# Wrapped spectra of a lag kernel, summed by accumulating transfers into DRAM in place of GpSimd copies and sums

## The chip, the cores and the metric

The kernel runs on one core of one Trainium2 chip. The metric is the device time of one execution in microseconds (us). A core has TensorE (PE; its weight loads are listed as PEld), VectorE (DVE), ScalarE (ACT), GpSimd (POOL) and SyncE (SP), each with an in-order queue of its own, and sixteen DMA engines that all queues share. SP and POOL issue the transfers here.

## The reference

A block of four residual layers over x (2048 positions, 512 channels): A, B, A, B, with the same weights in both rounds, each on a normalized input.

```python
def _A_ref(u, A_re, A_im, B_re, B_im, C_re, C_im, log_dt, Dskip):
    dt = jnp.exp(log_dt)[:, None]
    logdA = dt * (A_re + 1j * A_im)
    dB = dt * (B_re + 1j * B_im)
    P = jnp.exp(logdA[:, :, None] * l[None, None, :])      # 512 x 128 x 2048
    K = jnp.einsum("dn,dnl,dn->dl", C, P, dB).real         # the lag kernel, 512 x 2048
    # causal convolution of u with K along the positions, by FFTs of length 4096
    ...
    return y + u * Dskip

def _B_ref(x, w_gate, w_up, w_down):
    return (silu(x @ w_gate) * (x @ w_up)) @ w_down        # 512 -> 1376 -> 512

for _ in range(2):
    x = x + _A_ref(layernorm(x), ...)
    x = x + _B_ref(layernorm(x), ...)
```

## The kernel before, in words

**Blocks of 512 positions.** The convolution is cut into four blocks of positions (NB = 4) and the lag kernel into four parts of 512 lags. A block's spectrum has 512 complex values per channel, held as four quarters q of 128 (partitions), each with a real and an imaginary plane. Output block b is the sum over k = 0 to b of input spectrum b - k times the lag kernel's spectrum k. Because a product of two blocks of 512 spills into the next block, the lag spectrum that is used for k over 0 is a *wrapped* one: the spectrum of part k plus or minus the other plane of the spectrum of part k - 1 (real: subtract, imaginary: add, for the even quarters; the signs change places for the odd ones). Spectrum 0 is used as it is. It stays in SBUF in `w0r`; spectra 1 to 3 go to DRAM in `wdr` and are loaded again (L732) wherever a block needs them.

**The lag kernel by chunks of 64 channels.** There are eight chunks. For each, DVE and ACT make tables of powers (`gen_turns`, `gen_reduce`, `gen_trig`, `gen_exp`, `gen_mags`, `gen_e`) and a factor `g` (`gen_g`); the second half of g is finished by two accumulating transfers of 512 KB, issued by POOL into SBUF (L494, L499). PE multiplies tables and g into the lags of the chunk (`lags`, L509 and L510), ACT copies them out (`spread_in`, L515), PE spreads them over the partitions (`spread`), and ACT copies that out (L1001). Then `spectra` takes them through a transform on PE, one quarter after the other.

**`spectra`, where the change is made.** For a quarter with all four parts (k0 = 0, 29 times) PE writes `pw` (PSUM, tag sml, four buffers), ACT copies it to `s1` (L555; SBUF, tag uu, three buffers), POOL copies part 0 to `w0r` (L557) and makes the wrapped sums `wo` (L563, two operations; tag sg, two buffers), and SP stores each of the three parts to DRAM (L569). For three quarters of the last two chunks only part 0 is made first (ACT straight to `w0r`, L551) and parts 1 to 3 later (k0 = 1, three times; POOL's L566 and L567). The tag uu is also that of the early input spectra `u` (L289) and of the loaded input spectra `uu` in the blocks (L734); the tag sg is also that of the feed-forward's `sg`.

**Order.** The chunks run in a software pipeline that is written by hand: the functions are generators, and a loop over i (L958 to L1026) takes so many steps of each. For ACT, DVE and PE this order is kept as written (`manual_schedule`); SP's and POOL's instructions are placed by the scheduler when they are ready in its own timeline. In one turn of the loop, PE and ACT finish quarters 3 and 4 of chunk i - 1, the lags of chunk i, and quarters 1 and 2 of chunk i; DVE makes tables and g of the next chunks. Beside this, norms of the weights are summed: `st` is loaded (L314), squared by ACT (L316) and summed by PE (L320). Behind the loop come the last chunk, the first block's products (L736 to L741), the splitting of the weights (L626, L632) and the first norm (L202 to L207); then blocks of `ssm` and `ffn` alternate until the end.

The generator's steps are taken as `take(sp, n)`: one step is a quarter's products on PE, the next its copies and stores.

Of the kernel before, what the change touches and what calls it, by code (L numbers as in the profile page):

```python
# [15 lines left out]
AF = mybir.ActivationFunctionType  # L16
OP = mybir.AluOpType
# [5 lines left out]
P = 128  # L23
T = 512
NB = L // T
# [9 lines left out]
DC = 64  # L35
# [46 lines left out]
def kernel(ctx, tc, x, a_re, a_im, b_re, b_im, c_re, c_im, log_dt, d_skip,  # L82
                           w_gate, w_up, w_down, c_ef, c_ei, c_ek, c_am, c_eh, c_eih, out):
    nc = tc.nc
    V, A, G, PE = nc.vector, nc.scalar, nc.gpsimd, nc.tensor
# [9 lines left out]
    def tl(shape, name, tag, dt=F32):  # L95
        return sb.tile(shape, dt, name=name, tag=tag, bufs=BUFS[tag])

    def pbig(shape, name):
        return ps.tile(shape, F32, name=name, tag="big", bufs=2)

    def psml(shape, name):
        return ps.tile(shape, F32, name=name, tag="sml", bufs=4)
# [29 lines left out]
    w0r = sb.tile([P, 2, 4, 2, HD], F32, name="w0r")  # L132
# [19 lines left out]
    wdr = dram.tile([NB, 2, 4, P, 2, HD], F32, name="wdr")  # L152
# [139 lines left out]
    def second(h, q, space=psml):  # L292
        n = []
        for cp in range(2):
            t = tl([P, 2, HD], "n1", "w")
            nc.sync.dma_start(t, ndr[h, cp])
            n += [t[:, 0], t[:, 1]]
        return direct(1, h, q, n, space)
# [232 lines left out]
    def spectra(ch, kt, k0, k1, qs=QORD):  # L531


        h, off = ch // 4, (ch % 4) * DC
        nk = k1 - k0
        for q in qs:
            if k1 == 1:
                pw = pbig([P, 2, 8, 4, 16], "pw")[:, :, 0:1]
            elif k0 == 1:
                pw = pbig([P, 2, nk, 4, 16], "pw")  # L540
            else:
                pw = psml([P, 2, nk, 4, 16], "pw")
            for i, c in [(i, c) for c in range(4) for i in range(2)] if k1 == 1 else \
                        [(i, c) for i in range(2) for c in range(4)]:
                e = ek[q // 2][:, q % 2, c - 1, i] if c else ef[:, q, i]
                PE.matmul(pw[:, i], lhsT=e, rhs=kt[:, :, c + 4 * k0:4 * k1:4, :].rearrange("p g k d -> p k g d"), start=c == 0, stop=c == 3)  # L546
                if k0 == 1 and (i, c) == (0, 3):
                    yield
            yield
            if k1 == 1:  # L550
                A.activation(w0r[:, h, q, :, off:off + DC].rearrange("p i (g d) -> p i g d", g=4), pw[:, :, 0], AF.Copy)  # L551
                yield
                continue
            s1 = tl([P, 2, NB, 4, 16], "s1", "uu")
            A.activation(s1[:, :, :nk], pw, AF.Copy)  # L555
            if k0 == 0:
                G.tensor_copy(w0r[:, h, q, :, off:off + DC].rearrange("p i (g d) -> p i g d", g=4), s1[:, :, 0])  # L557
            sp, np_ = s1, NB - 1
            wo = tl([P, 2, NB - 1, 4, 16], "wo", "sg")
            ops = (OP.subtract, OP.add) if q % 2 == 0 else (OP.add, OP.subtract)  # L560
            for i in range(2):
                if k0 == 0:
                    G.tensor_tensor(wo[:, i], s1[:, i, 1:], s1[:, 1 - i, :3], ops[i])  # L563
                else:
                    w0s = w0r[:, h, q, 1 - i, off:off + DC].rearrange("p (g d) -> p g d", g=4)
                    G.tensor_tensor(wo[:, i, 0], s1[:, i, 0], w0s, ops[i])  # L566
                    G.tensor_tensor(wo[:, i, 1:], s1[:, i, 1:3], s1[:, 1 - i, :2], ops[i])  # L567
            for k in range(1, NB):
                nc.sync.dma_start(wdr[k, h, q, :, :, off:off + DC].rearrange("p i (g d) -> p i g d", g=4),  # L569
                                  wo[:, :, k - 1])  # L570
            yield


    def sizes(ch, kt, junk):

        A.activation(junk, kt, AF.Abs, accum_out=wsum[:, ch:ch + 1])
# [18 lines left out]
    def take(it, n):  # L595
        for _ in range(n):
            next(it, None)
# [301 lines left out]
    with tc.manual_schedule(engines={mybir.EngineType.Activation, mybir.EngineType.DVE, mybir.EngineType.PE}):  # L899
# [57 lines left out]
        sp = iter(())  # L957
        for i in range(NCH - 1):  # L958
# [46 lines left out]
            if more:  # L1005
                sp = spectra(i, kt, 0, NB)
                take(sp, 1)
                ex = gen_exp(i + 2, ts[i + 2])
                take(ex, 100)
                mags = gen_mags(i + 2, ts[i + 2])  # L1010
                take(mags, 2)
                norm_units(3, 9)
                take(sp, 2)
                norm_units(0, 0)
                take(mags, 2)
                take(sp, 2)
                sizes(i, kt, ks)
                take(ge, 4)
                take(gg, 1)
                while tops:  # L1020
                    tops.pop(0)()
                ts[i] = gs[i] = None
            else:
                sizes(i, kt, ks)
                take(ge, 4)
                take(gg, 1)  # L1026
# [9 lines left out]
        spec, ahead = inputs(), []  # L1036
        first = ssm(0, 0)
        sp = spectra(i, kt, 0, NB, QORD[:3])
        take(sp, 1)
        norm_units(4, 9)  # L1040
        take(sp, 2)
        norm_units(0, 0)
        take(sp, 3)
        last = spectra(i, kt, 0, 1, QORD[3:])
        ts[i] = gs[i] = None
        i = NCH - 1
# [7 lines left out]
        def split(hi, lo):  # L1054
            for _ in range(hi):
                his.pop(0)()
            for _ in range(lo):
                los.pop(0)()
# [7 lines left out]
        sp = itertools.chain(spectra(i, kts[1], 0, NB, QORD[:2]), spectra(i, kts[1], 0, 1, QORD[2:]))  # L1066
# [26 lines left out]
        take(rest, 3)  # L1093
        take(second(*sec[-1], space=pbig), 2)
        take(rest, 100)
        split(1, 0)
        take(first, 1)
        split(0, 1)
# [47 lines left out]
```

## Time and profile before

| | |
|---|---|
| median of 3 runs | 1188.11 us (1188.05 to 1190.89) |
| profiled execution | 1194.56 us, its span 1192.8 us |
| PE busy | 1108.3 us, 93% |
| DVE busy | 1026.5 us, 86% |
| ACT busy | 618.0 us, 52% |
| POOL busy | 185.0 us, 16% |
| mean granted TensorE clock | 0.983 |

The profile is of one execution. Busy times are sums over instructions; waiting isn't busy. "Released by" or an arrow behind an idle time names what the waiting instruction's semaphores waited for last. Times on POOL are rough. Of a transfer, the issue is an instruction of its queue (SPq, POOL), and the landing is when its last byte is told. Spans of the stages, by the lines that run in them: tables and first spectra from 0 to some 68 us, the loop over chunks to some 282 us, the last spectra, weights and first block's products to some 345 us, the blocks to 1192.8 us.

### The profile page before, as it was taken

The numbers are of one execution on the slowest core, as the hardware profiler recorded it, in microseconds if no ns is written. First come the engines' busy times: TensorE is split into PE (matmuls) and PEld (weight loads), VectorE is DVE, ScalarE is ACT, GpSimd is POOL, SyncE is SP. The second block draws the span as 40 slices with busy tenths as digits, with TensorE's granted clock in tenths as the row PEclk, the third lists the DMA queues.
The fourth block names the chain that finished last, engine by engine and source line by source line (L and its number), as shares of the span: only waits on it lengthen the run. The fifth ranks groups of instructions, "written<-read, shape, count | busy, mean of one in ns | idle before, by whom it ended". The sixth has DMA issues, their size and how long they took to land.

```text
span 1192.8 us, 25266 instructions
## 1 busy us (share of the span) xinstructions
PE 1108.3 (93%) x10268; PEld 861.2 (72%) x10268; DVE 1026.5 (86%) x1621; ACT 618.0 (52%) x1166; POOL 185.0 (16%) x238
## 2 busy tenths in 40 slices
PE   2889999889887989999999999999999999999998
PEld 2767776667875767768677787868687686867875
DVE  7989999997879999999999999999992899983211
ACT  6998887862355544537743523655432553224211
POOL 3105454343310011202100000211000010000000
PEclk9989999999989999999999999999999999999999
DMA  6444445577497326432344354324434134312000
GB/s 234 141 107 127 114 119 127 126 181 201 141 297 221 109 89 163 161 111 89 85 152 146 115 165 142 111 81 150 140 123 133 45 115 128 125 46 45 15 23 18
DMA packets 139031, 147.95 MB, mean 124 GB/s; under 512 B 77921, under 2 KB 87137, under 8 KB 138914
## 3 DMA queue, kind: packets, MB, share of 16 engines
q1 hardware_dynamic: 134050, 129.56, 35.8%
q0 software_dynamic: 4864, 16.78, 5.9%
q8 instruction: 80, 1.31, 0.5%
q14 instruction: 37, 0.30, 0.1%
HBM read 99.24 MB, written 28.31 MB: 107 GB/s over the span
## 4 chain that ended last, share of the span: by engine, by line
PE 35%; DVE 26%; issue 5%; ACT 3%; DMA 2%; POOL 2%; SPq 1%; DVEq 0%; ACTq 0%; POOLq 0%
PE pgu L860 6%; PE pgu L861 6%; PE pgu L862 6%; DVE t L736 4%; PE py L874 4%; PE py L875 4%; PE py L876 3%; DVE yk L739 3%; DVE yk L736 3%; PE pi L755 3%; PE pf L270 2%; DVE z L226 2%; DVE sg L866 2%; POOL rs L221 2%; DVE bt L226 1%
## 5 line engine op out<-in xcount | busy, mean ns | idle before, releaser
L860 PE MATMUL pgu<-mix,wsl 128*128 128x256 f16 x1280 | 350.2, 274 | 5.3 <-DVE sg L866 3.6
L862 PE MATMUL pgu<-mix,wsl 128*128 128x256 f16 x1280 | 350.3, 274 | 3.6 <-DVE wsl L632 3.6
L861 PE MATMUL pgu<-mix,wsl 128*128 128x256 f16 x1280 | 350.2, 274 | 0.0
L874 PE MATMUL py<-wsl,hh 128*128 128x512 f16 (+1 forms) x352 | 135.5, 385 | 8.9 <-DVE sgr L836 3.1
L861 PEld LDWEIGHTS <-wsl 128*128 128x128 f16 x1280 | 125.7, 98 | 21.8 <-issue 5.8
L862 PEld LDWEIGHTS <-wsl 128*128 128x128 f16 x1280 | 125.7, 98 | 19.1 <-DVE wsl L632 3.9
L860 PEld LDWEIGHTS <-wsl 128*128 128x128 f16 x1280 | 125.7, 98 | 15.8
L876 PE MATMUL py<-wsl,hl 128*128 128x512 f16 (+1 forms) x352 | 135.2, 384 | 1.3 <-DVE hl L868 1.3
L865 ACT ACTIVATE sg<-pgu,sc 128x512 f32<-128x512 f32 x80 | 54.5, 682 | 135.4 <-PE pgu L862 116.5
L736 DVE TENSOR_TENSOR t<-uu,w 128x1024 f32<-128x1024 f32 x96 | 117.0, 1219 | 8.2 <-DMA uu<-udr 7.9
L875 PE MATMUL py<-wsl,hh 128*128 128x512 f16 x320 | 123.3, 385 | 0.0
L739 DVE TENSOR_TENSOR yk<-yk,t 128x1024 f32<-128x1024 f32 x96 | 116.9, 1218 | 0.2
L866 DVE SCALAR_TENSOR_TENSOR sg<-pgu,sc,sg 128x512 f32<-128x512 f32 x80 | 59.7, 746 | 51.0 <-ACT sg L865 50.8
L546 PE MATMUL pw<-kt,ek 128*128 128x256 f32 (+2 forms) x420 | 98.6, 373 | 0.0
L755 PE MATMUL pi<-yl,mix 128*128 128x256 f16 x672 | 91.4, 273 | 1.7 <-ACT yl L744 1.4
L546 PEld LDWEIGHTS pw<-kt,ek 128*128 128x128 f32 x420 | 78.7, 195 | 9.5
L867 ACT ACTIVATE hh<-sg 128x512 f16<-128x512 f32 x80 | 50.0, 625 | 57.5 <-DVE sg L866 57.4
L221 POOL TENSOR_TENSOR rs<-mv,mhalf 128x2 f32<-128x2 f32 (+1 forms) x21 | 38.3, 1824 | 263.2 <-ACT mv L220 255.8
L270 PE MATMUL pf<-z,eh 128*128 128x256 f16 x576 | 74.6, 273 | 1.4 <-ACT z L260 1.4
L755 PEld LDWEIGHTS <-mix 128*128 128x128 f16 x672 | 65.2, 98 | 13.0 <-issue 2.0
L736 DVE TENSOR_TENSOR yk<-u,w0r 128x1024 f32<-128x1024 f32 x56 | 68.2, 1218 | 0.3 <-ACT u L272 0.3
L875 PEld LDWEIGHTS <-hh 128*128 128x128 f16 (+1 forms) x352 | 34.8, 99 | 46.2 <-issue 11.7
(240 smaller groups left out, 2245.8 us busy)
## 6 DMA issues: line engine op xcount, KB each, us to landing
w<-wdr SPq DMA_DIRECT2D x96, 256.0 KB, 2.7
uu<-udr SPq DMA_DIRECT2D x96, 256.0 KB, 3.0
udr<-u POOLq DMA_DIRECT2D x32, 256.0 KB, 2.9
wdr<-wo SPq DMA_DIRECT2D x96, 64.0 KB, 2.5
udr<-u SPq DMA_DIRECT2D x16, 256.0 KB, 2.2
g<-tmp POOLq DMA_DIRECT2D x8, 512.0 KB, 4.5
g<-btl POOLq DMA_DIRECT2D x8, 512.0 KB, 5.9
n<-ndr SPq DMA_DIRECT2D x16, 256.0 KB, 3.0
```

The source lines that it names most:

```text
L270: PE.matmul(pf[:, o], lhsT=e, rhs=m, start=k == 0, stop=k == len(terms) - 1)
L546: PE.matmul(pw[:, i], lhsT=e, rhs=kt[:, :, c + 4 * k0:4 * k1:4, :].rearrange("p g k d -> p k g d"), start=c == 0, stop=c == 3)
L736: V.tensor_tensor(t, uu.unsqueeze(1).to_broadcast([P, 2, 2, HD]), w.unsqueeze(2).to_broadcast([P, 2, 2, HD]), OP.mult)
L739: V.tensor_tensor(yk, yk, t, OP.add)
L755: PE.matmul(pi[:, o], lhsT=e, rhs=m, start=k == 0, stop=k == len(terms) - 1)
L860: PE.matmul(o, lhsT=wgu(wi, k, 0)[:, fs], rhs=nh[:, k], start=k == 0, stop=False)
L861: PE.matmul(o, lhsT=wgu(wi, k, 0)[:, fs], rhs=nlo[:, k], start=False, stop=False)
L862: PE.matmul(o, lhsT=wgu(wi, k, 1)[:, fs], rhs=nh[:, k], start=False, stop=k == 3)
L866: V.scalar_tensor_tensor(sg, pgu[:, 1], sc6[:, 4:5], sg, OP.mult, OP.mult)
L874: PE.matmul(py[:, r], lhsT=hh[:n, f, rc], rhs=wd(f, 0)[:n], start=f == 0, stop=False)
L875: PE.matmul(py[:, r], lhsT=hh[:n, f, rc], rhs=wd(f, 1)[:n], start=False, stop=False)
L876: PE.matmul(py[:, r], lhsT=hl[:n, f, rc], rhs=wd(f, 0)[:n], start=False, stop=f == FT - 1)
```

## The change

POOL's copies and sums go. ACT writes, beside `s1`, a negated copy `ng` of the plane that is to be subtracted. SP copies part 0 from `s1` into `w0r` and stores parts 1 to 3 of both planes to DRAM as they are (two transfers of 96 KB in place of three of 64 KB). Two accumulating transfers of 96 KB, issued by POOL, then add to the stored planes the other plane of the part before: one from `ng`, one from `s1`. They are written one quarter late (`wrapped(1)` leaves the latest quarter's pair for the next call), and what is left is written behind the last spectra. For k0 = 1, ACT copies part 0 from `w0r` into `s1` first.

```diff
             yield
+            w0s = w0r[:, h, q, :, off:off + DC]
+            wrapped(1)
             if k1 == 1:
-                A.activation(w0r[:, h, q, :, off:off + DC].rearrange("p i (g d) -> p i g d", g=4), pw[:, :, 0], AF.Copy)
+                A.activation(w0s.rearrange("p i (g d) -> p i g d", g=4), pw[:, :, 0], AF.Copy)
                 yield
                 continue
-            s1 = tl([P, 2, NB, 4, 16], "s1", "uu")
-            A.activation(s1[:, :, :nk], pw, AF.Copy)
-            if k0 == 0:
-                G.tensor_copy(w0r[:, h, q, :, off:off + DC].rearrange("p i (g d) -> p i g d", g=4), s1[:, :, 0])
-            sp, np_ = s1, NB - 1
-            wo = tl([P, 2, NB - 1, 4, 16], "wo", "sg")
-            ops = (OP.subtract, OP.add) if q % 2 == 0 else (OP.add, OP.subtract)
+            s1 = tl([P, 2, NB, DC], "s1", "uu")
+            ng = tl([P, NB - 1, DC], "ng", "sg")
+            j = q % 2
+            A.activation(s1[:, :, k0:].rearrange("p i k (g d) -> p i k g d", g=4), pw, AF.Copy)
+            if k0:
+                A.activation(s1[:, :, 0], w0s, AF.Copy)
+                A.activation(ng, s1[:, 1 - j, :3], AF.Copy, scale=-1.0)
+            else:
+                A.activation(ng.rearrange("p k (g d) -> p k g d", g=4), pw[:, 1 - j, :3], AF.Copy, scale=-1.0)
+                nc.sync.dma_start(w0s, s1[:, :, 0])
+            to = wdr[1:, h, q, :, :, off:off + DC].rearrange("k p i d -> p i k d")
             for i in range(2):
-                if k0 == 0:
-                    G.tensor_tensor(wo[:, i], s1[:, i, 1:], s1[:, 1 - i, :3], ops[i])
-                else:
-                    w0s = w0r[:, h, q, 1 - i, off:off + DC].rearrange("p (g d) -> p g d", g=4)
-                    G.tensor_tensor(wo[:, i, 0], s1[:, i, 0], w0s, ops[i])
-                    G.tensor_tensor(wo[:, i, 1:], s1[:, i, 1:3], s1[:, 1 - i, :2], ops[i])
-            for k in range(1, NB):
-                nc.sync.dma_start(wdr[k, h, q, :, :, off:off + DC].rearrange("p i (g d) -> p i g d", g=4),
-                                  wo[:, :, k - 1])
+                nc.sync.dma_start(to[:, i], s1[:, i, 1:])
+            wraps.append((to[:, j], ng, to[:, 1 - j], s1[:, j, :3]))
             yield

+    wraps = []
+
+    def wrapped(keep=0):
+        while len(wraps) > keep:
+            t0, f0, t1, f1 = wraps.pop(0)
+            G.dma_start(t0, f0, accum_op=OP.add)
+            G.dma_start(t1, f1, accum_op=OP.add)
...
         take(rest, 100)
+        wrapped()
         split(1, 0)
```

## The prediction

> **What bounds the kernel now.** I read the busy time of each engine in stretches of 20 to 40 us first, then the table of waits, then one turn of the loop over the chunks of lags, engine by engine in order of time. Columns of the stretches: length, then busy us and instructions of PE, PEld, DVE, ACT and POOL, granted clock, DMA share, GB/s; of the waits: engine and line, whom it waited for, us in total, times, longest.
>
> ```profile
> 130.27:161.30 31.03, 28.07 (x391) 21.79 (x390) 30.75 (x39) 26.14 (x43) 16.43 (x18) 1.00 0.47 114
> ...
> 290.00:310.00 20.00, 20.00 (x120) 18.42 (x119) 16.97 (x37) 5.77 (x9) 4.58 (x6) 1.00 0.37 124
> ...
> 341.00:420.00 79.00, 69.47 (x585) 53.73 (x586) 78.59 (x121) 39.31 (x72) 3.64 (x4) 0.94 0.64 203
> ...
> PE nrm L320 <- ACT sq L316: 9.3, 7, 1.7
> ...
> DVE im L388 <- ACT re L382: 0.8, 2, 0.4
> ```
>
> What the change touches runs ahead of 345 us; the instructions of the later blocks stay as they are. In a turn of the loop (130.27 to 161.30, 31.03 us) DVE is busy 30.75 us, PE 28.07, ACT 26.14. That looks like a DVE bound. But the waits show PE behind ACT seven times, once a chunk, and DVE too behind ACT (L388 on L382). So I followed one turn (start us, us, engine, line; in brackets the idle time before it):
>
> ```profile
> 130.27 1.02 ACT L515 ACTIVATE ks<-pk 128x1024 f32<-128x1024 f32 x1 [3.13 <-PE pk L510]
> ...
> 132.07 0.53 ACT L376 ACTIVATE xr<-xi 128x384 int32<-128x384 f32 x1
> ...
> 135.32 0.58 ACT L555 ACTIVATE s<-pw 128x512 f32<-128x512 f32 x1
> ...
> 149.62 1.23 ACT L316 ACTIVATE sq<-st 128x344 bf16<-128x344 f32 x3
> 150.75 0.58 ACT L555 ACTIVATE s<-pw 128x512 f32<-128x512 f32 x1
> ...
> 156.48 0.60 ACT L555 ACTIVATE s<-pw 128x512 f32<-128x512 f32 x1
> 156.95 1.25 ACT L316 ACTIVATE sq<-st 128x344 bf16<-128x344 f32 x3
> 161.30 1.02 ACT L515 ACTIVATE ks<-pk 128x1024 f32<-128x1024 f32 x1 [3.11 <-PE pk L510]
> ...
> 150.14 1.07 PE L320 MATMUL nrm<-sq,onesb 128*128 128x344 bf16 x3 [1.63 <-ACT sq L316]
> ...
> 155.46 0.36 PE L509 MATMUL pk<-re,g 128*32 128x64 f32 x7
> ...
> 148.86 0.86 POOL L499 DMA_DIRECT2D g<-btl  x1 [1.39 <-DVE btl L498]
> ...
> 129.78 1.21 DVE L450 TENSOR_TENSOR im<-im,re 128x1024 f32<-128x1024 f32 x1
> ...
> 132.90 0.55 DVE L385 TENSOR_TENSOR xi<-xi,xr 128x384 f32<-128x384 f32 x1
> ...
> 160.30 1.64 DVE L450 TENSOR_TENSOR im<-im,re 128x1024 f32<-128x1024 f32 x1
> ```
>
> The reader is to see a ring of ACT and PE. ACT runs without a gap over 0.1 us from the copy of the lags (L515, 130.27) to the squares (L316, done 150.85): 20.6 us. PE idles 1.63 us for those squares and then runs on to the next lags (L509 from 155.46), done when ACT starts L515 again at 161.30: 10.4 us. Sum 31.0, the whole turn; DVE is nowhere in it. DVE's g reaches PE through the transfer of L499, issued at 148.86 and landed 5.9 us later by the median below, at 154.8, when PE is busy with other products until 155.46. PE never waits for it. DVE hangs on the ring at L385 and L388, which need ACT's roundings: L376 is done at 132.60, L385 starts at 132.90. So DVE at 99% is a second engine that keeps pace, and what it gains it idles at L385. Behind the loop PE is full (20.00 of 20.00 us from 290).
>
> **The change, part by part.** Rows: POOL and ACT by shape (count, busy us, mean ns), SP's issues (min, median, max ns), landings (KB, median us), and SP's loads ahead of the stores.
>
> ```profile
> L563 POOL TENSOR_TENSOR wo<-s 128x192 f32<-128x192 f32 x58 | 56.2, 987 | 1.8 <-DMA wdr<-wo 1.6
> L557 POOL COPY w0r<-s 128x128 f32<-128x128 f32 x29 | 28.5, 982 | 57.4 <-ACT s L555 57.4
> ...
> L569 SPq DMA_DIRECT2D wdr<-wo x96: 512/611/1673, 94.4 to 334.9; - x96
> ...
> L290 SPq DMA_DIRECT2D udr<-u x16: 320/327/578, 35.7 to 337.7; - x16
> ...
> DMA to landing us min/median/max: 1.9/2.5/4.5
> ...
> uu<-udr SPq DMA_DIRECT2D x96, 256.0 KB, 3.0
> udr<-u POOLq DMA_DIRECT2D x32, 256.0 KB, 2.9
> ...
> g<-tmp POOLq DMA_DIRECT2D x8, 512.0 KB, 4.5
> g<-btl POOLq DMA_DIRECT2D x8, 512.0 KB, 5.9
> ...
> L555 ACT ACTIVATE s<-pw 128x384 f32<-128x384 f32 x3 | 1.5, 491 | 6.7 <-PE pw L546 6.7
> ...
> L551 ACT ACTIVATE w0r<-pw 128x128 f32<-128x128 f32 x3 | 0.8, 277 | 4.1 <-PE pw L546 2.6 <-PE pm L584 1.5
> ...
> 150.12 2.07 SPq L314 DMA_DIRECT2D st<-in_B_w_gate_dram  x3
> ```
>
> *POOL's copies and sums.* 29 copies (28.5 us) and 58 sums (56.2 us) go, with six pairs at the end. They slow DVE: L450 takes 1.64 us at 160.30 beside a sum of POOL and 1.21 at 129.78 alone. Over 80 to 310 us, the time of DVE instructions beside these operations above the shortest of their shape adds up to some 23 us (estimate from the order of time), 3.8 us a turn. It is hidden by the ring: gain taken 0. If the ring were shorter by 1 us, 1 us a turn of it would come through.
>
> *One more activation.* ng, 128x192 out of PSUM, 32 times. Between 277 ns for 128 elements and 491 ns for 384 that is 0.33 us. Of four a turn, those of the first three quarters come behind the squares that PE waits for and ahead of the 3.11 us that ACT idles before L515; they are hidden. That of the fourth (behind 135.32) lies in the gapless piece: 5 turns x 0.33 = +1.7 us. The three last quarters also copy w0r to s1 (0.28 each), in idle ACT.
>
> *SP.* Three stores of 256 runs become a copy of 256 runs into w0r and two stores of 384. Issue takes 327 ns for 128 runs (L290) and 611 for 256 (L569), so some 0.9 for 384: 2.4 us a quarter in place of 1.8, taken as 0, for the stores no longer wait for POOL. Only chunk 7's w0r is read soon after it is written, by DVE, while PE is full; without that cover a copy that lands late costs what it is late.
>
> *POOL's new queue.* 64 accumulating issues of 96 KB, by L499 (0.86 us) 55 us of POOL, in place of 85 and the six pairs. Queued behind one that waits for its store are the transfers of g (L499 goes out 13.5 us behind the fourth quarter's L555) and two memsets; PE would wait for g, DVE for both. POOL isn't kept in written order: the memset of L407, written behind L499, runs 18 us ahead of it (130.19),
>
> ```profile
> 130.19 0.21 POOL L407 MEMSET re<- 128x64 f32 x1 [1.96 <-PE pk L510]
> ```
>
> so an accumulation will stand where its store has landed, not where the deferral by one quarter writes it.
>
> *The new wait.* s1 has three buffers and ng two, and both are now held until an accumulation has landed. The third quarter's ng (ACT, behind 156.48) needs the first quarter's buffer. From the start of the first L555 (150.75): 0.58 for it, 0.86 until SP has issued the weight loads ahead of it (to 152.19), 0.61 for the w0r copy, 0.3 for the longer issue, 2.5 for the store to land, then POOL's issue to landing. No accumulation into DRAM is in the trace; the nearest rows are 2.9 (same queue, plain, to DRAM), 4.5 and 5.9 (accumulating, five times the bytes, to SBUF). I take 4.5, for it accumulates: sum 9.35 us. ACT has until 161.30 - 1.25 (squares) - 0.33 = 159.72, which is 8.97 behind 150.75, before L515 is late. So 0.4 us x 6 third quarters = +2.4. Ends: with 1.9 to land and 2.9, no delay; with 4.5 (the longest store) and 5.9, 12.75, 3.8 us a turn, +23.
>
> By the Trainium skill, "DMA: Bandwidth & Descriptors", Anatomy of one DMA (SWDGE path), such a transfer takes 2.0 us and its bytes at 436 GB/s, 2.2 us here, and the sum would be without the 2.4, at 1186.9 (estimate from that page). The accumulating g<-tmp (4.5) is longer than the 3.2 which the page gives for 512 KB.
>
> *The end.* Here the change shortens a chain:
>
> ```profile
> 330.48 0.49 ACT L555 ACTIVATE s<-pw 128x384 f32<-128x384 f32 x1 [2.23 <-PE pw L546]
> ...
> 333.58 0.45 POOL L567 TENSOR_TENSOR wo<-s 128x128 f32<-128x128 f32 x1
> ...
> 333.64 1.84 SPq L569 DMA_DIRECT2D wdr<-wo  x3
> ...
> 336.23 0.86 SPq L734 DMA_DIRECT2D uu<-udr  x2
> ...
> 341.38 1.22 DVE L736 TENSOR_TENSOR t<-uu,w 128x1024 f32<-128x1024 f32 x1 [7.94 <-DMA uu<-udr]
> ...
> 349.80 1.22 DVE L736 TENSOR_TENSOR t<-uu,w 128x1024 f32<-128x1024 f32 x1
> ...
> 344.22 0.40 PE L862 MATMUL pgu<-mix,wsl 128*128 128x256 f16 x1 [3.62 <-DVE wsl L632]
> ...
> 323.89 1.32 PE L801 MATMUL pt<-ident,nn 128*128 128x128 f32 x5 [3.33 <-ACT nn L799]
> ```
>
> SP's stores of the last quarter wait for POOL (done 334.03), and behind them is the load of uu for which DVE stands idle 7.94 us and, through it, PE 3.62 us. Without POOL, SP can issue them at 331.1, behind the L555 that ends at 330.97; two of 0.9 and the 0.75 that lie between store and L734 today (335.48 to 336.23) bring L734 to 333.7: -2.5 us, which passes on, as DVE is full from there (78.59 of 79.00 us from 341 to 420).
>
> The first uu takes the buffer of the quarter before, 10 us earlier. Late next is the second uu: it now waits for the last accumulation (331.1 + 1.8 + 2.5 + 4.5, about 340, and lands by 345), and DVE needs it 8.42 us behind the first, at 347.3. DVE's chain into L204 loses POOL's slowing: -0.4 (an estimate from the order of time).
>
> Sum: +1.7 + 2.4 - 2.5 - 0.4 = +1.2 us on the profiled execution (span 1192.8, 1194.56 us with what lies around it). The median of the runs, 1188.11, is 6.4 below that, and I put the sum on it: 1189.3.
>
> **The rivals.** *ACT waits for the accumulations (slower).* The same wait, with an accumulation into DRAM in 256-byte runs as slow as g<-btl or slower, or one placed on POOL behind the memset that waits for the lags. It decides from 8.97 us on. For it: each step of that chain has a longer row; against it: five times fewer bytes. 1.7 + 23 - 2.9 = +22, about 1210; half-way, 1198.
>
> *DVE was the bound (faster).* DVE's 30.75 of 31.03 us speaks for it, PE's place-fixed waits and L385's against. All 23 us back on the forecast: 1189.3 - 23, about 1166. By the Trainium skill, "SBUF — State Buffer", SBUF: two separate sides, a GpSimd operation and a DVE operation with two SBUF inputs exclude each other on a shared port for whole instructions, so a DVE-bound stage would gain. The trace agrees on the contention (1.64 against 1.21 us) and shows the loss to be less than a whole POOL operation (987 ns).
>
> *Only the end counts (faster).* No stall in the loop, and uu, issued at 333.7, lands in its median 3.0 us and not in 5.1: DVE goes on at 336.7, 4.7 earlier. 1188.1 + 1.7 - 4.7 - 0.4, about 1185. Against it: the same big loads are in flight then.
>
> *POOL's queue at the end.* Two accumulations of the first of the three last quarters (0.86 each, and a wait for their store) stand ahead of L204, the norm whose end sets PE's 3.33 us wait: +2.5, about 1192.
>
> **How the numbers follow.** A difference under 0.3% (3.6 us) can hardly be told from none here. Forecast (1185 to 1194) 0.52: 0.02 faster, 0.40 same, 0.10 slower. ACT waits, 0.28, slower. DVE bound, 0.08, faster. Only the end, 0.08, halved between faster and same. POOL's queue, 0.04, halved between same and slower. So faster 0.14, same 0.46, slower 0.40. The range leaves out the DVE bound and the worst tenth of the waits: 1183 to 1210.
>
> **What would show it.** Right: DVE's L450 all near 1.22 us; DVE's busy time per turn 27 us with 3 to 4 us idle, ended by ACT's L376 or L382; turns of 31.3 to 32 us; ACT's wait for pk still 2 to 3 us; DVE's wait for uu 5.5 us. Wrong: turns under 30 us (DVE was the bound); an idle ACT ahead of ng put down to the accumulating transfer, and turns over 33 us; POOL's g transfers issued late behind an accumulation.

## The result, and the profile after

The changed kernel takes 1207.7 us (median of 6 runs, 1201.7 to 1210.6), the kernel before 1190.3 in the same comparison (6 runs, 1188.1 to 1192.7): 1.4% slower, ratio 1.0141 (95% interval 1.0107 to 1.0175). The profiled execution has a span of 1208.5 us and took 1210.28. The two profiled executions took 4.2 us (before) and 2.6 us (after) more than the medians.

Where the 15.7 us between the two spans (1208.5 and 1192.8) arise is read at equal amounts of PE's work. First both kernels' stretches from the start to the 3600th and to the 8000th matmul in order of time (columns as in the prediction: length, then busy us and instructions of PE, PEld, DVE, ACT and POOL, clock, DMA share, GB/s). Before:

```profile
0.00:365.74 365.74, 308.77 (x3604) 248.62 (x3605) 331.95 (x475) 260.91 (x478) 127.31 (x170) 0.96 0.58 162
0.00:910.00 910.00, 833.79 (x8003) 652.92 (x8004) 858.30 (x1359) 526.75 (x993) 177.28 (x228) 0.98 0.48 142
```

After, with two turns of the loop, the last turn (from the copy of chunk 6's lags to that of chunk 7's), and the same 79 us behind 341 that the prediction showed:

```profile
0.00:374.60 374.60, 309.82 (x3607) 249.35 (x3608) 306.36 (x472) 269.88 (x512) 117.84 (x135) 0.95 0.83 174
0.00:925.90 925.90, 837.49 (x8003) 656.14 (x8004) 835.18 (x1359) 535.59 (x1028) 166.47 (x193) 0.97 0.59 148
99.97:133.83 33.86, 29.70 (x388) 22.40 (x388) 28.27 (x39) 27.48 (x48) 11.60 (x12) 0.95 0.87 151
133.83:165.87 32.04, 28.41 (x393) 22.08 (x392) 28.08 (x38) 27.06 (x47) 15.72 (x17) 1.00 0.88 146
264.78:297.00 32.22, 24.32 (x368) 19.47 (x368) 21.57 (x34) 8.98 (x19) 12.44 (x11) 0.95 1.11 222
341.00:420.00 79.00, 73.10 (x602) 58.68 (x603) 72.59 (x108) 48.81 (x84) 9.03 (x8) 0.94 0.83 235
```

The first six turns take 196.6 us (68.22 to 264.78) in place of 187.7, +8.9. The last turn takes 32.22 in place of 26.16, +6.1. From there to the 3600th matmul 5.6 us come back: that matmul ends at 374.6 in place of 365.7, +8.9 in all. And 6.7 are lost again behind it: the 8000th ends at 925.9 in place of 910.0, and the last matmul 15.6 later. DVE has less to do in every turn (28.08 us of 32.04, before 30.75 of 31.03), and the turn is longer all the same.

The table of waits of the changed kernel (engine and line, whom it waited for, us in total, times, longest) shows where the engines stood:

```profile
POOL wdr L577 <- DMA wdr<-s: 91.7, 12, 15.3
...
DVE xi L385 <- ACT xr L376: 24.6, 6, 5.0
ACT ng L564 <- DMA wdr<-ng: 22.4, 8, 9.3
...
PE nrm L320 <- ACT sq L316: 13.5, 8, 2.5
...
POOL wdr L577 <- ACT s L561: 13.9, 1, 13.9
...
PE pk L509 <- DMA g<-btl: 10.3, 2, 5.4
...
DVE mix L812 <- ACT mix L810: 7.4, 1, 7.4
```

DVE now idles at L385 behind ACT's rounding, 5.0 us at most, as the ring said it would: what DVE gains it waits away. ACT waits 22.4 us in eight places for an accumulation to free the buffer of a negation. PE's wait for the squares has grown from 9.3 us in seven places to 13.5 in eight. And POOL stands over 90 us waiting for stores, with all that is queued behind.

ACT in the turn from 133.83 (start us, us, engine, line; in brackets the idle time before it and who ended it):

```profile
153.48 1.24 ACT L316 ACTIVATE sq<-st 128x344 bf16<-128x344 f32 x3
154.61 0.58 ACT L559 ACTIVATE s<-pw 128x512 f32<-128x512 f32 x1
...
160.33 0.60 ACT L559 ACTIVATE s<-pw 128x512 f32<-128x512 f32 x1
164.51 0.33 ACT L564 ACTIVATE ng<-pw 128x192 f32<-128x192 f32 x1 [3.57 <-DMA wdr<-ng]
...
165.87 1.01 ACT L515 ACTIVATE ks<-pk 128x1024 f32<-128x1024 f32 x1
```

The third quarter's negation (164.51) waits 3.57 us for the first quarter's accumulation, until 9.90 us behind the first L559 (154.61). The prediction's chain came to 9.35, with 8.97 allowed. ACT has no idle time left ahead of L515 (165.87; before, 3.11 us), and so L515 is late, though by little: it starts 0.48 us behind the end of PE's last product of the lags (165.39), before the change some 0.1. The pieces of the chain, from the lines themselves (min, median and max in ns, then in us from issue to landing): POOL's accumulation of ng, then SP's stores:

```profile
L577 POOL DMA_DIRECT2D wdr<-ng x32: 1264/1298/2871, 93.6 to 352.2; - x32
...
DMA to landing us min/median/max: 3.4/4.6/10.5
```

```profile
DMA to landing us min/median/max: 2.0/3.3/8.1
```

The accumulation of ng lands 4.6 us behind its issue in the median (taken: 4.5) and 10.5 at most (that of s1: 5.1 and 10.7), a store 3.3 (taken: 2.5). The accumulation's issue takes 1.30 us (POOL's share was taken at 0.86).

The last turn, on POOL, and then the end of the same queue, ahead of the norm L204:

```profile
278.15 1.28 POOL L577 DMA_DIRECT2D wdr<-ng  x1 [9.71 <-DMA wdr<-s]
...
279.73 1.94 POOL L494 DMA_DIRECT2D g<-tmp  x1
280.33 2.23 POOL L499 DMA_DIRECT2D g<-btl  x1
...
335.90 1.29 POOL L577 DMA_DIRECT2D wdr<-ng  x1 [13.95 <-ACT s L561]
...
338.58 0.19 POOL L204 TENSOR_SCALAR rs<-mv 128x2 f32<-128x2 f32 x1
```

DVE has the second product of chunk 7's g ready at 273.13, but its transfer is issued at 280.33, behind an accumulation (278.15) that waits 9.71 us for a store. That store is chunk 5's fourth quarter, issued by SP at 269.55 to 270.85. PE starts the last lags 4.89 us late for it, and g<-btl has landed 8.8 us behind its issue. Issued behind DVE's product at some 273.3, it would have landed by 282.1 with the same 8.8 us, ahead of 284.36, where PE begins to wait (an estimate from these rows):

```profile
289.25 0.45 PE L509 MATMUL pk<-re,g 128*32 128x64 f32 x3 [4.89 <-DMA g<-btl]
```

The norm: DVE is done with L203 at 333.47, POOL starts L204 at 338.58, behind two accumulations. Before, it followed DVE at once (POOL in the kernel before):

```profile
319.48 0.78 POOL L204 TENSOR_SCALAR rs<-mv 128x2 f32<-128x2 f32 x1 [1.99 <-DVE mv L203]
```

### The profile page after: what moved, and what is told of

It is laid out like the page before. It is cut to its first block, busy times and chain, and to the rows that moved or that the text cites. A ratio compares the mean times of both kernels' runs of the same rounds, so it can differ in the third digit from the quotient of the medians.

```text
span 1208.5 us, 25301 instructions
## 1 busy us (share of the span) xinstructions
PE 1111.9 (92%) x10268; PEld 864.4 (72%) x10268; DVE 1003.5 (83%) x1621; ACT 626.8 (52%) x1201; POOL 174.6 (14%) x203
## 2 busy tenths in 40 slices
DMA packets 172007, 156.15 MB, mean 129 GB/s; under 512 B 110897, under 2 KB 120113, under 8 KB 171890
## 4 chain that ended last, share of the span: by engine, by line
PE 46%; DVE 24%; ACT 13%; DMA 8%; issue 6%; SPq 2%; POOL 1%; ACTq 0%; DVEq 0%; POOLq 0%
PE pgu L866 7%; PE pgu L867 7%; PE pgu L868 7%; PE pi L761 4%; PE py L880 4%; PE py L881 4%; PE py L882 4%; PE pw L546 4%; DVE t L742 4%; DVE yk L745 3%; PE pf L270 3%; DMA wdr<-s 2%; DVE z L226 2%; DVE yk L742 2%; DVE sg L872 2%
## 5 line engine op out<-in xcount | busy, mean ns | idle before, releaser
L866 PE MATMUL pgu<-mix,wsl 128*128 128x256 f16 x1280 | 351.9, 275 | 11.1 <-DVE sg L872 5.4
L868 PEld LDWEIGHTS <-wsl 128*128 128x128 f16 x1280 | 126.2, 99 | 15.7
L761 PEld LDWEIGHTS <-mix 128*128 128x128 f16 x672 | 65.4, 98 | 11.1
L577 POOL DMA_DIRECT2D wdr<-ng x32 | 54.5, 1704 | 125.0 <-DMA wdr<-s 91.7
L750 ACT ACTIVATE yl<-mix,sy 128x512 f16<-128x512 f32 x56 | 40.2, 719 | 56.9 <-DVE mix L747 56.5
```

Of the source, the lines that this page charges most:

```text
L761: PE.matmul(pi[:, o], lhsT=e, rhs=m, start=k == 0, stop=k == len(terms) - 1)
L866: PE.matmul(o, lhsT=wgu(wi, k, 0)[:, fs], rhs=nh[:, k], start=k == 0, stop=False)
L868: PE.matmul(o, lhsT=wgu(wi, k, 1)[:, fs], rhs=nh[:, k], start=False, stop=k == 3)
```

## The experiments

In the table, "loop" is the first six turns in the profiled execution; "slowed" counts, among the turns two to six, those with a mean granted clock of 0.95, all the others having 1.00; "last turn" is the seventh. Clocks and turns are those of one execution each (that of all_three took 4 us more than its median). Medians are of 6 to 12 runs; they come from three comparisons, in which the kernel before had 1190.7, 1190.5 and 1189.3, so kernels of different comparisons are better compared by their ratios. The kernels without accumulations, and no_accum_chunk6, do not compute the whole result.

| kernel | median us | ratio to before (95%) | loop us | slowed | last turn us |
|---|---|---|---|---|---|
| before | 1190.3 | | 187.7 | 1 | 26.2 |
| changed | 1207.7 | 1.011 to 1.018 | 196.6 | 3 | 32.2 |
| no_accum | 1193.1 | 0.999 to 1.003 | 190.3 | 1 | 27.5 |
| no_accum_no_ng | 1193.4 | 0.9995 to 1.004 | 189.4 | 1 | 28.3 |
| ng_four_slots | 1204.0 | 1.007 to 1.013 | 191.0 | 2 | 29.9 |
| no_accum_chunk6 | 1207.8 | 1.010 to 1.016 | 195.3 | 3 | 30.6 |
| late_order | 1205.6 | 1.009 to 1.016 | 195.8 | 3 | 32.8 |
| pool_pinned | 1206.4 | 1.009 to 1.016 | 197.2 | 4 | 31.0 |
| all_three | 1199.7 | 1.005 to 1.011 | 197.2 | 4 | 30.6 |
| all_three_dve | 1200.6 | 1.005 to 1.012 | 186.9 | 0 | 34.6 |
| ng4_g_first | 1202.1 | 1.008 to 1.014 | 193.0 | 3 | 31.6 |
| ng4_g_first_dve | 1199.0 | 1.005 to 1.011 | 187.4 | 0 | 33.0 |
| no_accum_ng_thrice | 1201.0 | 1.007 to 1.012 | 197.4 | 4 | 26.2 |
| new_at_end | 1199.6 | 1.006 to 1.010 | 188.6 | 1 | 25.3 |

### Without the accumulations

```
-            t0, f0, t1, f1 = wraps.pop(0)
-            G.dma_start(t0, f0, accum_op=OP.add)
-            G.dma_start(t1, f1, accum_op=OP.add)
+            wraps.pop(0)
```

> The 64 accumulations are left out (wdr keeps the unsummed spectra); the stores, the copies and the negations stay, and PE, ACT and DVE run the same instructions in the same order up to 345 us. Theory (the loss lies in the accumulations: ACT's wait for the negations' two buffers, and the transfers of g and the norm L204 queued on POOL behind accumulations that wait for their stores; what is left is the negation's 0.33 us in the ring, +1.7 to +2, and the earlier uu, -2.5 to -5): 1187 us, 1184 to 1191, turns 30.5 to 31.5. Rival DVE was the bound (its 23 us come through once the new waits are gone): 1167 to 1172, turns near 28. Rival ACT's added work (all four negations a turn count, 1.4 us x 6 turns, and the waits cost nothing): 1196 to 1199, turns near 32.5.

Measured: 1193.1 us, 14.6 less than the changed kernel, and no different from the kernel before. Two turns of it, and the first line of its page:

```profile
161.90:193.46 31.56, 27.78 (x390) 21.67 (x389) 28.04 (x39) 27.06 (x47) 1.79 (x4) 1.00 0.54 130
258.32:285.83 27.51, 23.17 (x370) 18.28 (x368) 22.05 (x34) 8.77 (x17) 1.74 (x2) 1.00 0.82 220
```

```profile
PE 1107.6 (93%) x10268; PEld 860.8 (72%) x10268; DVE 1002.8 (84%) x1621; ACT 625.9 (53%) x1201; POOL 93.9 (8%) x139
```

DVE is busy 1002.8 us, 23.7 less than before (1026.5), with nothing on POOL to slow it, no accumulation to wait for, and 28.04 us of work in a turn of 31.56. The time does not fall. At full clock its turns take 31.6 us (without the negations as well, below, 31.4) against 31.2 before, with 2.7 us less for DVE to do in a turn: DVE did not set the turn. And 14.6 of the 17.4 us of loss go with the accumulations and all that waits for them; which of these it is, the next runs were to tell. The median is 6 us above the expected 1187: in the profiles part of it is the last turn (27.5 us, +1.3) and the loop (+2.6), part the blocks behind (5.8 us from the 4400th to the 8000th matmul, below).

### Without the negations as well

```
-            ng = tl([P, NB - 1, DC], "ng", "sg")
-                A.activation(ng, s1[:, 1 - j, :3], AF.Copy, scale=-1.0)
-                A.activation(ng.rearrange(...), pw[:, 1 - j, :3], AF.Copy, scale=-1.0)
```

> Accumulations and negations are both left out; the stores and copies stay. Beside the kernel without accumulations it prices the 32 negations. Theory: only the fourth quarter's negation lies in the ring of ACT and PE, so 1.7 to 2.0 us less than without accumulations alone, about 1185. Rival ACT's added work: all four a turn count, about 8 us less. Rival DVE was the bound: no difference between the two, both near 1167.

Measured: 1193.4, the same. In turns at full clock the profile shows 31.39 us (mean of four) against 31.61 (four) with the negations: 0.2 a turn, near the forecast 0.33 and far from the 1.4 of "all four count". Six times 0.2 is less than these medians can tell. Nor does the clock tell the two apart: one of five turns is slowed in each, and the mean granted clock over all twelve executions is 0.986 in both, as in the kernel before beside them.

### Four slots for the negations

```
-            ng = tl([P, NB - 1, DC], "ng", "sg")
+            ng = ngs[len(turn) % 4]; turn.append(q)
+    pair = [tl([P, 2, NB - 1, DC], f"ng{i}", "sg") for i in range(2)]
+    ngs = [pair[0][:, 0], pair[1][:, 0], pair[0][:, 1], pair[1][:, 1]]
```

> The whole computation; the negations rotate through four slots (two in each of the two buffers they had) in place of two; PE, ACT, DVE and SP keep their order of instructions. Theory: ACT no longer waits 3.6 us for the third quarter's slot, the loop of six turns gets back 1.0 to 1.3 a turn: 1207.7 - 7 = about 1201 (1199 to 1203); the last turn's loss and that of L204 stay. Rival ACT's added work, and rival contention (the 256-byte packets slow all other transfers): no change, 1207 to 1208.

Measured: 1204.0, 3.7 less; expected 7. The wait itself is gone: its table of waits has no row of ACT behind wdr<-ng, and the third quarter's negation follows its copy. The profiled loop is 5.6 us shorter. A turn at full clock and a slowed one:

```profile
130.31:161.68 31.37, 28.08 (x391) 21.79 (x390) 28.19 (x38) 27.03 (x48) 15.39 (x17) 1.00 0.99 157
226.53:259.78 33.25, 30.06 (x391) 23.01 (x390) 29.84 (x40) 27.09 (x47) 12.55 (x12) 0.95 0.94 164
```

At full clock the turns of ng_four_slots, all_three and ng4_g_first (six turns) take 31.4 us, those of the kernels with two slots (changed, no_accum_chunk6, late_order, pool_pinned: seven) 31.9. So the wait costs 0.5 us a turn, 3 us in all, and the prediction's 0.4 was nearly right. But the row of 226.53 shows a second thing, which no theory so far had: 33.25 us at a clock of 0.95, with nobody waiting for an accumulation.

### The clock: one negation three times

```
-                A.activation(ng..., pw[:, 1 - j, :3], AF.Copy, scale=-1.0)
+                for _ in range(3 if q == QORD[3] and ch < NCH - 2 else 1): A.activation(ng..., scale=-1.0)
```

> The kernel without accumulations (1193.1), with the fourth quarter's negation made three times in place of once in the loop's six turns (2 x 0.33 us more in ACT's gapless piece; the other quarters as they are). It is to separate the ring from the clock. Ring alone: +0.66 a turn, +4, about 1197, clock 1.00 in most turns. Ring and clock: PE's idle time ahead of the squares' product (L320) grows from 1.93 to 2.6 us; in the ten profiles so far 10 of 11 turns with 2.0 us or more there had a clock of 0.95 and lasted 2 us longer, against 10 of 38 turns below: +4 and 3 to 4 more slowed turns of 2 us, about 1204 (1201 to 1206). Rival, ACT isn't in the ring: no change, 1193.

Measured: 1201.0, +7.9 (the two medians are of different comparisons; by the ratios it is nearer 10); the ring alone gives +4. Four of its five middle turns are slowed (33.3 to 33.9 us), the fifth takes 32.34. In one of them, PE's wait for the squares, then the stretches of 2 us behind it, a slowed turn, and the full-clock one:

```profile
120.85 1.39 PE L320 MATMUL nrm<-sq,onesb 128*128 128x512 bf16 x3 [2.60 <-ACT sq L316]
```

```profile
120.00:122.00 2.00, 1.15 (x3) 0.35 (x3) 1.10 (x2) 2.00 (x5) 0.00 (x0) 0.71 0.93 163
122.00:124.00 2.00, 2.00 (x6) 1.40 (x5) 2.00 (x4) 1.26 (x3) 0.00 (x0) 0.50 0.88 261
124.00:126.00 2.00, 2.00 (x10) 1.70 (x10) 2.00 (x6) 1.91 (x5) 0.00 (x0) 0.94 0.56 128
167.10:200.51 33.41, 29.75 (x391) 23.06 (x390) 28.03 (x39) 27.79 (x50) 2.07 (x5) 0.95 0.50 122
233.88:266.22 32.34, 28.39 (x391) 21.85 (x390) 29.01 (x40) 27.74 (x49) 2.07 (x4) 1.00 0.57 143
```

Behind PE's idle 2.60 us the granted clock falls to half for some 3.4 us: (0.29 + 0.50 + 0.06) x 2 us = 1.7 us of PE's time lost, on the piece of PE that the ring runs over. Over the fourteen profiles (seventy turns), by PE's idle time ahead of L320 (in each of the thirty slowed turns the clock is halved once, for 3.41 us, from 0 to 2.1 us behind the start of L320):

| idle ahead of L320 | turns | of them slowed | mean turn at full clock | slowed |
|---|---|---|---|---|
| 1.16 to 1.29 us (DVE copies the fourth quarter) | 10 | 0 | 31.4 | |
| 1.63 to 1.76 (no negations in the ring: before, new_at_end, no_accum_no_ng) | 15 | 3 | 31.3 | 32.6 |
| 1.88 to 2.00 (one negation) | 30 | 14 | 31.7 | 33.5 |
| 2.14 to 3.08 (three negations, or ACT late) | 15 | 13 | 32.0 | 33.6 |

This run lengthened ACT's work ahead of that idle time and nothing else. Its median, too, lies 4 us above what the ring gives, and its mean clock over six executions is 0.983, against 0.988 of the kernel before beside it; the two kernels that shorten the idle time (below) have no slowed turn among ten. So a longer idle time is enough to bring the drops. For the single negation of the change it isn't shown: in the third row 13 of 26 turns are slowed in the kernels that accumulate and 1 of 4 in no_accum, whose clock and median are those of the kernel without negations. What the accumulations add at the same idle time stays open; the mean clock over all executions is 0.979 to 0.984 in the ten kernels that accumulate and 0.986 in no_accum. Five turns of one execution are few for each kernel; the grouping over all seventy is what the reading rests on. By the Trainium skill, "TensorE: Matmul & The Clock Gate", Part 1 (The HAM clock gate), the array's clock is halved by a monitor that looks at PE's business in free-running windows of 3413 ns. The length of the drop agrees. The rule in the section "HAM oscillation" of the same page of the Trainium skill, that PE should have no idle gaps above some 3.4 us, is too mild for this trace: with gaps of 2.1 to 3.1 us there was a drop in 13 of 15 turns.

### DVE copies the fourth quarter (with the repairs below)

```
+            j, dv = q % 2, ch < NCH - 2 and q == QORD[3]
+            (V.tensor_copy if dv else lambda o, i: A.activation(o, i, AF.Copy))(s1[:, :, k0:]..., pw)
+                ... if not dv else V.tensor_scalar(ng..., pw[:, 1 - j, :3], -1.0, None, OP.mult)
```

> As the kernel with the three repairs, and in the six turns of the loop DVE copies the fourth quarter's spectra out of PSUM and negates them in place of ACT (0.58 and 0.33 us of ACT's gapless piece behind L515; DVE idles 3 to 4 us a turn). Theory, the ring of ACT and PE sets the turn: 0.9 us x 6 less than the kernel with the three repairs, about 5, near 1183. Rival DVE is as near to the bound as ACT: no gain or 1 to 3 us more. Rival, the turn hangs on PE alone: no change.

Measured: 1200.6, no less than all_three (1199.7). But the loop is shorter than before the change, 186.9 us, with no slowed turn, and PE's idle time ahead of the squares is 1.2 us:

```profile
149.51 1.06 PE L320 MATMUL nrm<-sq,onesb 128*128 128x344 bf16 x3 [1.23 <-ACT sq L316]
```

```profile
130.05:161.32 31.27, 28.07 (x391) 21.79 (x390) 29.34 (x42) 26.35 (x46) 14.82 (x18) 1.00 1.01 158
255.45:290.07 34.62, 25.83 (x370) 20.63 (x368) 25.56 (x39) 7.95 (x15) 13.48 (x11) 0.89 1.06 206
```

The ring theory asked for 0.9 us a turn: at full clock it is 0.2 (31.27 against 31.47, the one such turn of all_three), for PE now idles elsewhere. What the move brings in the loop is the clock. It is lost again behind it: the last turn takes 34.62 us with a mean clock of 0.89, and over all executions the mean clock is 0.983 in both kernels.

### POOL's queue: a pair left out, and ties of order

Left out, chunk 6's first three quarters:

```
-            wraps.append((to[:, j], ng, to[:, 1 - j], s1[:, j, :3]))
+            wraps.extend([(to[:, j], ng, to[:, 1 - j], s1[:, j, :3])] if ch != NCH - 2 or k0 else [])
```

> The six accumulations of chunk 6's first three quarters alone are left out, those that stand on POOL ahead of the last chunk's g transfers; PE, ACT, DVE and SP keep their order, and on POOL the norm L204 moves ahead of the accumulations that are left. Theory (POOL's queue): the last turn falls from 32.2 to about 26.5 us, and L204 follows DVE again: 6 + 3 to 5 less, 1197 to 1202. Rival contention: the accumulating traffic is only 6 of 64 transfers smaller, so 1 to 2 us less, about 1206.

Measured: 1207.8, no change. The expectation had the wrong pair: in its trace the transfers of g still stand behind an accumulation that waits 7.66 us, that of chunk 5's fourth quarter, and L204 still starts 4.7 us behind L203, behind accumulations that are left. Six transfers less changed nothing.

Tied behind what is written ahead:

```
-            t0, f0, t1, f1 = wraps.pop(0)
+            ch, *pairs = wraps.pop(0)
+            for t, f in pairs:
+                (tc.keep_in_program_order if ch >= NCH - 2 else id)(G.dma_start(t, f, accum_op=OP.add))
```

> The whole computation. The accumulations of the chunks 6 and 7 are tied on POOL behind what is written ahead of them (edges of order, no waits), so that the g transfers of the last chunk and the norm L204 to L207 go ahead of them; the later blocks keep the order of the changed kernel. Theory (POOL's queue): the last turn falls from 32.2 to 26.5-28 us and L204 follows DVE's L203 at once: 4 to 6 and 3 to 5 less, 1197 to 1201. Rival contention (the traffic of the accumulations, not their place in the queue, delays g and the norm): 1206 to 1208, the last turn still over 30 us.

Measured: 1206.4, 1.3 less; expected 7 to 11. POOL in this kernel:

```profile
279.29 1.28 POOL L578 DMA_DIRECT2D wdr<-ng  x1 [8.29 <-DMA wdr<-s]
...
280.88 1.94 POOL L494 DMA_DIRECT2D g<-tmp  x1
...
334.66 0.77 POOL L204 TENSOR_SCALAR rs<-mv 128x2 f32<-128x2 f32 x1 [11.18 <-DVE mv L203]
```

Of L204 the tie did what it should: DVE's L203 ends at 334.56 and L204 follows after 0.1 us, not 5.1. In the profile the kernel ends 1.6 us earlier; but a single drop of the clock costs as much (1.7), so what the tie brings to the end isn't shown. Of g it did nothing: the pair in front (279.29) is chunk 5's. A second try began the ties at that quarter:

```
+    held = [(c, q) for c in range(NCH - 3, NCH) for q in QORD][3:]
+                (tc.keep_in_program_order if (ch, q) in held else id)(G.dma_start(...))
```

> The whole computation: four slots for the negations, and on POOL the accumulations are tied behind what is written ahead of them from the fourth quarter of chunk 5 on, for the runs before showed that it is this quarter's pair (not chunk 6's) that stands ahead of the last chunk's g and waits 8 us for its store. L204 to L207 go ahead too; the later blocks keep the order of the changed kernel. Beside the kernel with four slots alone (1204.0, last turn 29.9 us, L204 3.7 us behind L203). Theory (place in POOL's queue): L494 goes out at once behind DVE, last turn 27 to 28 us, L204 at once: about 1199 (1197 to 1201). Rival traffic (the transfers land late wherever they stand): last turn still 29.5 to 30.5, about 1202 to 1204.

Measured: 1202.1, against 1204.0 for the four slots alone; beside their own kernels before the two are alike (1.011 and 1.010). The last turn stayed at 31.6 us, and the same pair still stands in front of L494 (POOL waits 9.30 us there and issues L494 at 276.02; DVE's product was done at 268.20): the edge seems to bind an accumulation only to the POOL instruction written just ahead of it, and that is another accumulation, itself free. So the run doesn't separate place from traffic. With DVE copying the fourth quarter:

> The same, with DVE copying and negating the fourth quarter in the six turns of the loop, and the order of the kernel before from the second later block on. Beside all_three_dve (1200.6; its loop took 186.9 us against 187.7 before, none of its five middle turns fell to a clock of 0.95, its last turn took 34.6 us behind the late g). Theory, queue and ring: the loop stays at 187 us with the clock at 1.00, the last turn falls to 27 to 29 us: about 1194 (1191 to 1197). Rival traffic: the last turn stays over 31 us, 1198 to 1201.

Measured: 1199.0; loop 187.4, again no slowed turn in five, last turn 33.0, the g transfers late in the same way. With a ratio of 1.008 it is no better than all_three or all_three_dve: 0.8% above the kernel before is the best that the kernels with accumulating transfers reached.

### The order of the later blocks

```
+    keep_order(tc, nc.cur_bb.bb.instructions[cut:])
```

keep_order binds each engine's instructions, from the second block on, to the order in which the kernel before was compiled.

> The whole computation. From the second block of the later part on (behind some 430 us) every engine issues its instructions in the order in which the kernel before issues them; ahead of that the order of the changed kernel stays. Theory (the compiled order of the later blocks came out otherwise, and it costs 6 to 7 us: at DVE's 450th instruction the changed kernel is 9.8 us behind the kernel before and at its end 15.6; at 600 us DVE stands 4.3 us for a product that PE now does later): 1207.7 - 6.5 = about 1201 (1199 to 1203). Rival, order costs nothing and the later loss follows from the later start: 1207 to 1208.

Measured: 1205.6, 2.1 less, within the spread of the medians; expected 6.5. In the profile, up to the 3600th, 4400th and 8000th matmul:

```profile
0.00:374.50 374.50, 310.11 (x3606) 249.55 (x3607) 306.00 (x472) 269.91 (x512) 117.75 (x135) 0.95 0.85 175
0.00:489.40 489.40, 411.78 (x4403) 325.07 (x4404) 419.31 (x657) 323.74 (x615) 125.17 (x146) 0.95 0.77 167
0.00:921.10 921.10, 836.54 (x8004) 656.19 (x8005) 835.91 (x1359) 536.33 (x1028) 162.66 (x193) 0.97 0.60 149
```

At the 3600th it is 8.8 us behind the kernel before, at the 4400th (before: 474.9) 14.5, at the 8000th 11.1. So the forced order loses 5.7 where it begins and then gives 3.4 back, where the changed kernel's own order lost 7.0 from the 3600th to the 8000th. It takes the later loss away and puts another in its place; what the order costs by itself is not settled. So it is in all five profiles with the forced order of the kernel before: they lose 3.9 to 7.0 us from the 3600th to the 4400th matmul and none from there to the 8000th. The other eight, those without accumulations among them, lose 4.4 to 7.2 from the 4400th to the 8000th. The later loss, then, does not come from the accumulations; in the changed kernel and in no_accum, 3.4 us of it are clock (5.1 us lost there to a lower clock, 1.7 in the kernel before).

Together:

> The whole computation with the three repairs together: four slots for the negations, the accumulations of the chunks 6 and 7 tied behind g and L207, and the order of the kernel before from the second later block on. Theory: nothing is left of the loss but the negation in the ring (+2 to +3 over the loop) and a last turn 1 us longer, against uu's 5 to 7 us: 1190.5 + 4 - 6.5 = about 1188 (1185 to 1192), and the repairs add up, each at its own price. Rival (the losses hide one another, or accumulating traffic costs by itself): 1196 to 1200. Rival DVE was the bound: 1170.

Measured: 1199.7, 8.0 less than the changed kernel: near the upper rival. The junction costs 6.5 us here too (from the 4000th to the 4400th matmul).

### The new path for the last three quarters alone

On the kernel before; copies, negation and stores there as in the change, all else with POOL's sums:

```
+            if k0:
+                s1, ng = tl([P, 2, NB, DC], "s1", "uu"), tl([P, NB - 1, DC], "ng", "t1")
+                ...
+                wraps.append(((to[:, j], ng), (to[:, 1 - j], s1[:, j, :3])))
```

> The kernel before with one part of the change: only the three last quarters (those that lack their first block at first) take the new path, their negations in a buffer of their own kind, their accumulations tied behind L207 on POOL; all other quarters keep POOL's copies and sums, and the later blocks the order before. Theory: nothing changes up to the last quarters, and the load of uu no longer waits for POOL behind the stores: DVE's wait of 7.9 us shrinks by 4 to 7: 1190.5 - 5 = about 1185 (1183 to 1188). Rival (what is gained there is idled away behind it, or the first uu waits for another buffer): 1189 to 1191.

Measured: 1199.6, 9 to 10 us slower than before, in place of 5 faster. Its waits from 320 to 345 us:

```profile
DVE mix L824 <- ACT mix L822: 11.5, 1, 11.5
...
PE pt L819 <- ACT nn L817: 10.1, 1, 10.1
...
ACT ng L559 <- DMA wdr<-ng: 8.2, 1, 8.2
```

Loop and last turn are those of the kernel before. One negation waits 8.2 us for an accumulation to free its buffer, ACT's step of the norm is queued behind it, and PE and DVE stand 10 to 11 us. The repair met the fault that it was to avoid, at another place. But the wait isn't shown to be the whole loss: in the profile the kernel is 5.8 us behind the kernel before at the 3400th matmul, 1.9 ahead at the 3600th, and 4.4 behind at the 4400th, behind the start of the forced order, like the others that have it. How the loss divides between the wait and that order stays open. The load of uu goes out at 340.11 here (before: 336.23), so what an earlier uu would gain was not measured.

## Why the prediction failed where it did

The forecast was 1189.3 and no change; the measured 1207.7 is the rival "ACT waits for the accumulations" in its time (about 1210), though the wait that it named made a fifth of the loss (3.7 of 17.4 us by the four slots). That rival's 1210 came from a wait that costs 3.8 us in every turn, and it cost 0.5; that the time fell near it, and inside the range of 1183 to 1210, is luck. What is shown is that 14.6 of the 17.4 us go when the accumulations go. The step that failed is the price of 0 for POOL's queue; beside it, the sum has no term for the clock.

- *POOL's copies and sums, gain 0.* Right, by no_accum: 23.7 us of DVE's time gone, none of the kernel's, and no shorter turn at full clock (31.6 us, before 31.2). The rival at 1166 is out.
- *One more activation, +1.7.* In size right or a little high (0.2 us a turn at full clock where 0.33 was taken; without accumulations the medians with and without the negations are the same, 1193.1 and 1193.4). But the sum lacks a term beside it: no part of the prediction asked what an idle PE does to its clock, though the profile before had a turn at 0.95 (32.66 us, the others 31.0 to 31.4). The negation lengthens PE's idle time ahead of the squares from some 1.7 to 1.94 us. With accumulations half of such turns were slowed (13 of 26; 3 of 15 in the kernels without negations in the loop), 1.3 to 1.8 us each. That the negation by itself brings this isn't shown, for no_accum has it and no more slowed turns than before.
- *The new wait, +2.4.* The mechanism and nearly the size: 9.90 us for the chain of 9.35; 0.5 us a turn at full clock for 0.4; 3.7 us by the four slots. Its pieces came out longer at the issue (1.30 for 0.86) and the store (3.3 for 2.5). ACT being late then lengthens PE's idle time in the next turn to 2.3 to 3.1 us, and such a turn is mostly slowed as well.
- *POOL's new queue, 0.* This step failed: "an accumulation will stand where its store has landed". POOL's order is fixed when the kernel is compiled, by a model's times. On the chip the store landed 8 us behind its issue, and g, L204 and PE waited: last turn +6.1, L204 +5.0. The prediction had named both (g among the signs of a miss, L204 as a rival at +2.5 with a chance of 0.04), and gave them too little. How much of the norm's 5.0 us reaches the end isn't shown: pool_pinned takes it away and is 1.3 us faster, within the spread. Of the last turn, PE's 4.89 us behind g are the place in the queue by the estimate above, and the store that the queue waited for was itself late (8 us, 3.3 in the median); no run separates place from traffic. Without accumulations L499 goes out 0.3 us behind DVE and the turn takes 27.5 us.
- *SP at the end, -2.5.* The sign was right: DVE's wait of 7.9 us for uu is 0.3 now, and from the last turn to the 3600th matmul 5.6 us come back, though L204 is late. The size isn't shown, for 3.4 of them are clock: over that stretch the kernel before lost 6.8 us to a lower clock (0.92 in the mean), the changed kernel 3.4 (0.96).
- *"The instructions of the later blocks stay as they are."* They do, but their order doesn't: it is compiled from modelled times, and 6.7 us are lost behind the 3600th matmul, 3.0 in no_accum. That the order is the cause isn't shown: the order of the kernel before, forced on the changed one, takes the later loss away and costs 5.7 us where it begins.

## What to carry to other kernels

A sum moved from an engine into an accumulating transfer holds its source buffer for the store's landing, the queue's wait and its own landing (here 9.9 us from the copy out of PSUM, where 1 us of GpSimd had done): give it as many buffers as that takes, or the engine that fills them stops. On a queue in fixed order, a transfer that waits for another transfer does not belong ahead of anything that PE will need (here POOL stood 9.7 us behind one store, and PE 4.9 us behind POOL). And before adding an instruction to the chain that PE idles for, look at how near that idle time is to where the granted clock drops: here a gap of 1.9 us in place of 1.7 went, in kernels that accumulate, with twice the share of slowed turns (13 of 26 against 3 of 15), and each cost 1.3 to 1.8 us.

## What the runs showed of the hardware

- PE's granted clock drops to 0.50 for 3.41 us, at idle gaps shorter than that: in 0 of 10 turns with a gap of 1.2 us, 3 of 15 with 1.7, 14 of 30 with 1.9 to 2.0, 13 of 15 with 2.1 to 3.1 us.
- An accumulating transfer of 96 KB into DRAM in 256-byte runs lands 4.6 to 5.1 us behind its issue in the median and 10.7 at most (those into SBUF, five times as large, 4.6 and 5.3 in the median), and its issue of 384 runs holds POOL 1.3 us.
- With the change the bytes that the DMA engines move grow little (147.95 to 156.15 MB; without the accumulations 149.85) and the packets by a quarter (139,031 to 172,007; without, 146,406).
